# First FFT of a filter-and-FFN kernel: both banks of a stage A pair filled ahead of their copies, four units of F placed ahead of stage B, W_out behind z on the queue

## The chip, the core and the metric

One core of a Trainium2 chip. The metric is the device time of one execution in microseconds (us), as the median of several runs. A "span" is the time from the first to the last instruction of one profiled execution; it is 1 to 2 us shorter than the device time. The program runs on one core only. Ratios are the mean time of one kernel's fast runs over the mean time of the fast runs of the kernel before in the same rounds, with a 95% interval. They are therefore not quite the ratio of the medians that are quoted beside them. Different calls ran on different chips, so medians of different calls are compared only roughly.

Names in the views: tiles that begin with ps lie in PSUM (psA, psT, psB, psP, psY: stage A, the transposes, stages B, P and Y; psf: F being spread; psH, psO: the FFN's first and second product). uT and ut are stage A's result before and after the transposes, ze the copies of stage P's result, dZ is z in DRAM, zt is z as it is read back, xw is x. A slot is one step of the FFN loop; a y unit is one of the pieces in which stage Y is done.

## The reference

```python
def _attn_ref(x, filt_r, filt_i):            # x: (8, 3008, 256), filt: (1505, 256)
    X = np.fft.rfft(x, axis=1)
    Y = X * (filt_r + 1j * filt_i)[None]
    return np.fft.irfft(Y, n=3008, axis=1)

def _moe_ref(x, w_in, w_out):                # x: (24064, 256), w_in: (256, 2048)
    h = np.maximum(x @ w_in, 0.0)
    return h * h @ w_out
```

The output of the first is the input of the second. The FFT along 3008 = 64 x 47 points is done by matmuls in stages. Stage A transforms along 47, stage B along 64. The product with the filter F follows, then the inverse stage P, whose result z goes through DRAM to be rearranged, then the inverse stage Y. The FFN then reads y.

## The kernel before

The FFTs of batches 1 to 7 are woven into the FFN loop of the batch ahead of them. The FFT of batch 0 can't be: it stands alone ahead of the loop, with the loads of the weights and the first loads of batch 1. The change touches only this prologue. Its parts, with cuts marked by "...":

```python
p_prod = ctx.enter_context(tc.tile_pool(name="p_prod", bufs=3))
...
sPF = p_prod.tile([128, 6, 128], F16, tag="prod", name="sPF")   # the placement matrix of F
...
def chunk_a0(c):                                   # stage A of batch 0
    for k in range(2):
        banks, groups = bank_pair(...)             # psH: one tile of two banks; psF, psO: two tiles
        for dt in range(2):
            ps = banks[dt]
            for i in range(4):
                ...                                # two matmuls of 96 columns
            ...                                    # then the copy of this bank to uT
...
for c in (0, 2, 1, 3):
    chunk_a0(c)
...                                                # casts of F on GpSimd, casts of W_in
for k in range(6):
    turn_u(k)                                      # transposes psT, copies to ut
    if k > 2:
        place_f(0, k - 3, ...)                     # F spread over the partitions, in psH
place_f(1, 0, nc.scalar)
for r in range(14):
    if r < 12:
        unit_b(0, r)                               # stage B into psF, product with F (VectorE)
    ...                                            # the other eight place_f, on ScalarE
    if r >= 2:
        unit_p(0, r - 2)                           # stage P, copy to ze; every third: write of z
    for k in {4: (0, 1), 7: (2,)}.get(r, ()):
        load_wide(1, k)                            # x of batch 1, 1 MB each
        cast_wide(1, k, nc.gpsimd, nc.gpsimd)
    if r == 10:
        read_z(0, 0, (0,))                         # first half of the z that y units 0 to 3 need
        load_wout(0)                               # 1 MB
        for k in range(2):
            cast_wout(k, nc.gpsimd)
read_z(0, 0, (1,))                                 # the second half: needs all four z writes
read_z(0, 1)
for c in (0, 2, 1):
    chunk_a(1, c)                                  # stage A of batch 1
load_wout(1)
...
for n in range(4):
    unit_y(0, n)                                   # stage Y; the FFN loop starts after it
```

All DMAs shown are issued from one sequencer (SP), in program order: what stands behind a DMA that has to wait, waits too.

## Time and profile before

| | before |
|---|---|
| device time, median of the first 4 runs | 817.5 us (814.8 to 818.6) |
| span of the profiled run | 817.4 us (this execution took 819.15 us) |
| TensorE busy | 785.9 us (96%) |
| FFN loop starts (first psH matmul) | 65.55 us |
| the FFN's first second product (first psO matmul) | 77.4 us |
| last z write issued, landed | 49.69, 60.19 us |

The prediction shows the lines that carry the argument. One more view belongs beside them, the timeline of the DMA queue's sequencer (start, us, engine and line, destination<-source, number of issues). "Landed" times, here and below, are the trace's own records of when a DMA's completion semaphore reached its full count.

```profile
36.95 0.38 SPq L471 DMA_DIRECT2D dZ<-ze  x1
37.43 1.25 SPq L220 DMA_DIRECT2D xw<-in_x_dram  x2
40.50 0.38 SPq L471 DMA_DIRECT2D dZ<-ze  x1
45.42 0.33 SPq L220 DMA_DIRECT2D xw<-in_x_dram  x1
45.84 0.39 SPq L471 DMA_DIRECT2D dZ<-ze  x1
48.46 0.34 SPq L484 DMA_DIRECT2D zt<-dZ  x1
48.89 0.75 SPq L316 DMA_DIRECT2D wout<-in_moe_w_out_dram  x1
49.69 4.25 SPq L471 DMA_DIRECT2D dZ<-ze  x1
60.21 1.25 SPq L484 DMA_DIRECT2D zt<-dZ  x3
```

The reader is to see the order: the loads of x right behind the first z write, and W_out between the third z write (45.84) and the last.

### The profile page before, as it was taken

The numbers are of one execution on the slowest core, as the hardware profiler recorded it, in microseconds if no ns is written. First come the engines' busy times: TensorE is split into PE (matmuls) and PEld (weight loads), VectorE is DVE, ScalarE is ACT, GpSimd is POOL, SyncE is SP. The second block draws the span as 40 slices with busy tenths as digits, with TensorE's granted clock in tenths as the row PEclk, the third lists the DMA queues.
The fourth block names the chain that finished last, engine by engine and source line by source line (L and its number), as shares of the span: only waits on it lengthen the run. The fifth ranks groups of instructions, "written<-read, shape, count | busy, mean of one in ns | idle before, by whom it ended". The sixth has DMA issues, their size and how long they took to land.

```text
span 817.4 us, 14776 instructions
## 1 busy us (share of the span) xinstructions
PE 785.9 (96%) x6102; PEld 554.1 (68%) x6102; DVE 552.7 (68%) x896; ACT 554.1 (68%) x709; POOL 21.9 (3%) x26
## 2 busy tenths in 40 slices
PE   7858899999999999999999999999999999999998
PEld 4734666667767676776668667776767667676666
DVE  5744699459965699557985599656995579653442
ACT  2736576677767677676776767777776767766663
POOL 3330000000000000000000000000000000000000
PEclk9998999999999999999999999999999999999999
DMA  9686356445572555424572455715555242421111
GB/s 365 230 251 176 123 142 163 96 109 165 146 174 59 162 155 138 121 78 142 155 198 62 108 167 145 175 59 163 152 142 116 78 142 79 118 63 39 40 40 52
DMA packets 88092, 108.10 MB, mean 132 GB/s; under 512 B 6241, under 2 KB 78817, under 8 KB 83553
## 3 DMA queue, kind: packets, MB, share of 16 engines
q1 hardware_dynamic: 87816, 107.01, 46.2%
q8 instruction: 48, 0.79, 0.4%
q10 hardware_dynamic: 144, 0.15, 0.1%
q14 instruction: 20, 0.16, 0.1%
q0 software_dynamic: 64, 0.00, 0.0%
HBM read 58.90 MB, written 48.23 MB: 131 GB/s over the span
## 4 chain that ended last, share of the span: by engine, by line
PE 85%; DMA 9%; DVE 3%; ACT 2%; issue 0%; POOL 0%; SPq 0%; ACTq 0%; POOLq 0%
PE psO L547 36%; PE psH L532 35%; DMA dZ<-ze 3%; DMA zt<-dZ 3%; PE psY L502 3%; PE psA L349 3%; PE psB L431 2%; PE psP L466 2%; DMA ut<-dU 1%; DMA xw<-in_x_dram 1%; DVE prod L434 1%; PE warm L267 1%; DVE h L540 1%; PE psf L283 0%; PE psf L286 0%; PE psA L392 0%
## 5 line engine op out<-in xcount | busy, mean ns | idle before, releaser
L536 ACT ACTIVATE h<-psH 128x1024 f16<-128x1024 f32 x376 | 384.9, 1025 | 193.8 <-PE psH L532 193.8
L532 PE MATMUL psH<-yt,sWin 128*128 128x512 f16 (+7 forms) x1728 | 388.3, 352 | 2.9 <-DVE yt L511 2.3
L547 PE MATMUL psO<-sWout,h 128*128 128x256 f16 x3008 | 388.6, 272 | 0.0
L547 PEld LDWEIGHTS <-h 128*128 128x128 f16 x3008 | 290.6, 98 | 77.8
L540 DVE TENSOR_TENSOR h<-h 128x1024 f16<-128x1024 f16 x376 | 254.2, 685 | 106.3 <-ACT h L536 104.9
L532 PEld LDWEIGHTS <-sWin 128*128 128x128 f16 x1728 | 159.7, 98 | 104.0 <-issue 6.4
L434 DVE TENSOR_TENSOR prod<-psB,sF 128x1024 f16<-128x1024 f32 x96 | 116.7, 1220 | 10.4 <-PE psB L431 7.2
L511 DVE CAST yt<-psY 128x376 f16<-128x376 f32 x64 | 35.0, 549 | 63.3 <-PE psY L502 57.5
L468 ACT CAST ze<-psP 128x512 f16<-128x512 f32 x96 | 55.9, 585 | 22.8 <-PE psP L466 19.4
L355 DVE CAST u<-psA 96x512 f16<-96x512 f32 x50 | 34.3, 687 | 47.9 <-PE psA L349 45.1
L554 ACT COPY ost<-psO 128x512 f32<-128x512 f32 x94 | 55.4, 590 | 8.1 <-PE psO L547 6.4
L502 PE MATMUL psY<-sC,zt 112*128 112x94 f16 x512 | 42.8, 207 | 8.0 <-DMA zt<-dZ 7.7
L502 PEld LDWEIGHTS <-zt 112*128 112x128 f16 x512 | 35.1, 99 | 20.3 <-DMA zt<-dZ 7.7
L431 PE MATMUL psB<-ut,sSB 128*128 128x256 f16 x192 | 36.6, 272 | 2.3 <-DVE prod L434 1.2
L448 DVE TENSOR_TENSOR yf<-prod,yf 128x512 f16<-128x512 f16 x84 | 35.7, 425 | 2.9
L349 PE MATMUL psA<-x,sC 94*96 94x512 f16 x96 | 36.6, 382 | 0.0
L509 ACT CAST yt<-psY 128x376 f16<-128x376 f32 x64 | 29.9, 468 | 7.5 <-issue 6.5
L431 PEld LDWEIGHTS <-sSB 128*128 128x128 f16 x192 | 18.6, 98 | 23.5 <-issue 4.8
L466 PE MATMUL psP<-yf,sSP 128*128 128x256 f16 x168 | 32.1, 273 | 1.8 <-DVE prod L434 1.6
L328 DVE CAST x<-x 94x2048 f16<-94x2048 f32 x24 | 29.2, 1216 | 0.0
L353 ACT CAST u<-psA 96x512 f16<-96x512 f32 x50 | 28.6, 572 | 0.0
L441 DVE COPY yf<-prod 64x512 f16<-64x512 f16 x84 | 24.3, 290 | 2.9
(59 smaller groups left out, 231.6 us busy)
## 6 DMA issues: line engine op xcount, KB each, us to landing
x<-in_x_dram SPq DMA_DIRECT2D x20, 768.0 KB
dZ<-ze SPq DMA_DIRECT2D x32, 384.0 KB
zt<-dZ SPq DMA_DIRECT2D x64, 192.0 KB
dU<-u SPq DMA_DIRECT2D x28, 384.0 KB
out_dram<-ost SPq DMA_DIRECT2D x32, 256.0 KB
out_dram<-ost SPq DMA_DIRECT2D x64, 128.0 KB
ut<-dU SPq DMA_DIRECT2D x7, 1024.0 KB
xw<-in_x_dram SPq DMA_DIRECT2D x6, 1024.0 KB
```

Source lines behind the costliest of these rows:

```text
L349: nc.tensor.matmul(ps[0:96, :], sSA, x16s[(b, c)][:, m, :], start=True, stop=True)
L431: nc.tensor.matmul(ps[:, i * D:(i + 1) * D], sSB[:, 2 * p + i, :], uts[b][:, 2 * p + i, :], start=True, stop=True)
L434: nc.vector.tensor_mul(out=prod, in0=ps.rearrange("p (a d) -> p a d", d=D).unsqueeze(1).to_broadcast([128, 2, 2, D]), in1=sF[:, :, 2 * p:2 ...
L448: nc.vector.tensor_add(out=yf, in0=prod[:, 0], in1=yf)
L466: nc.tensor.matmul(ps[:, i * D:(i + 1) * D], sSP[:, c2, :], prod[:, i, :], start=True, stop=True)
L468: nc.scalar.copy(out=zes[(b, c)][:, 2 * i6:2 * i6 + 2, :], in_=ps.rearrange("p (a d) -> p a d", d=D))
L502: nc.tensor.matmul(ps[:, 94 * jj:94 * jj + 94], zt[:, 4 * (g % 2) + jj, dt * 128:(dt + 1) * 128], sSY, start=True, stop=True)
L532: nc.tensor.matmul(ps[:, i, o:o + n], sWin[:, dt, jt * 128:(jt + 1) * 128], yts[b][:, dt, r:r + n], start=(dt == 0), stop=(dt == 1))
L536: nc.scalar.activation(out=h2[:, 2 * s:2 * s + 2, :], in_=ps, func=AF.Relu)
L540: nc.vector.tensor_mul(out=v, in0=v, in1=v)
L547: nc.tensor.matmul(pso[g][:, t % 2, :], h2s[g][:, jt, t * 128:(t + 1) * 128], sWout[:, jt, :], start=(jt == 0), stop=(jt == NJT - 1))
L554: nc.scalar.copy(out=ost, in_=pso[g])
```

## The change

It has three parts. **Banks:** in stage A of batch 0 all matmuls of a pair come first, then its two copies. **F:** the transposes 4 and 5 use the smaller PSUM tiles so that psH is free for F, four units of F are placed after the transposes and ahead of stage B (three before; these are units of F's real part, and one of its imaginary part is placed there in both kernels), f_i and the identity matrix are loaded earlier, and VectorE takes one of the casts of F. **Queue:** the first load of batch 1's x is issued ahead of stage B, and W_out is loaded after the last z read that the first y units need, with all its casts on VectorE. The core of the diff (the new column numbers of the constants are left out):

```diff
-    nc.sync.dma_start(out=sPF, ...); nc.sync.dma_start(out=sC0[:, 576:1472], ...)
-    load_f(1)
+    load_f(1)
+    nc.sync.dma_start(out=sPF, ...); nc.sync.dma_start(out=sC0[:, 704:1472], ...)
@@ chunk_a0
             for dt in range(2):
-                ps = banks[dt]
                 for i in range(4):
                     ...                                    # matmuls into banks[dt]
+            for dt in range(2):
                 ...                                        # copy of banks[dt]
@@ turn_u
+        if k > 3:
+            npair[0] = k - 2                               # psF, psO in place of psH
@@ W_out's casts in the FFN loop
-            for k in range(2, 4):
-                put(2 + k, 1, cast_wout, k, nc.vector)
+            for k in range(4):
+                put(3 + k, 1, cast_wout, k, nc.vector)
@@ prologue
     for k in range(6):
         turn_u(k)
-        if k > 2:
-            place_f(0, k - 3, nc.vector if k % 2 else nc.scalar)
+    nc.vector.tensor_copy(out=f16s[0][:, 1, e1], in_=f32s[1][:, e1])
+    for k in range(4):
+        place_f(0, k, nc.vector if k % 2 else nc.scalar)
     place_f(1, 0, nc.scalar)
+    load_wide(1, 0)
+    cast_wide(1, 0, nc.gpsimd, nc.gpsimd)
     for r in range(14):
         ...
-        for k in {4: (0, 1), 7: (2,)}.get(r, ()):
+        for k in {4: (1,), 7: (2,)}.get(r, ()):
             ...
         if r == 10:
             read_z(0, 0, (0,))
-            load_wout(0)
-            for k in range(2):
-                cast_wout(k, nc.gpsimd)
     read_z(0, 0, (1,))
+    for k in range(2):
+        load_wout(k)
     read_z(0, 1)
     for c in (0, 2, 1):
         chunk_a(1, c)
-    load_wout(1)
```

Lines behind the change have numbers higher by two in the new kernel: the product is L434 before and L436 after.

More of the change, by code (lines that the diff above doesn't have):

```diff
@@ L103, in _build_consts @@
     C0[:, 0:576] = S0.reshape(128, 6, 2, 2, NC).transpose(0, 1, 4, 2, 3).reshape(128, 576)
-    C0[:, 896:1472] = S0.reshape(128, 576)
-    C0[0:94, 576:672] = SA.reshape(94, 96)
-    C0[:, 672:766] = SY.reshape(128, 94)
-    C0[:, 768:896] = np.eye(128)
+    C0[:, 576:704] = np.eye(128)
+    C0[:, 704:1280] = S0.reshape(128, 576)
+    C0[0:94, 1280:1376] = SA.reshape(94, 96)
+    C0[:, 1376:1470] = SY.reshape(128, 94)
     return f16(C0, 128), f16(PF, 128), f16(SB, 128), f16(SP, 128), f16(SPx, 128)
@@ L203 @@
     sC0 = const.tile([128, 1472], F16, name="sC0")
-    nc.scalar.dma_start(out=sC0[:, 0:576], in_=dC0.ap()[:, 0:576])
+    nc.scalar.dma_start(out=sC0[:, 0:704], in_=dC0.ap()[:, 0:704])
     s0 = sC0[:, 0:576].rearrange("p (w q) -> p w q", q=96)
-    s1 = sC0[:, 896:1472].rearrange("p (w q) -> p w q", q=96)
-    sSA = sC0[0:94, 576:672]
-    sSY = sC0[0:112, 672:766]
-    ident = sC0[:, 768:896]
+    s1 = sC0[:, 704:1280].rearrange("p (w q) -> p w q", q=96)
+    sSA = sC0[0:94, 1280:1376]
+    sSY = sC0[0:112, 1376:1470]
+    ident = sC0[:, 576:704]
     sPF = p_prod.tile([128, 6, 128], F16, tag="prod", name="sPF")
@@ L243 @@
     load_f(0)
+    load_f(1)
     nc.sync.dma_start(out=sPF, in_=dPF.ap().rearrange("p (w q) -> p w q", q=128))
-    nc.sync.dma_start(out=sC0[:, 576:1472], in_=dC0.ap()[:, 576:1472])
-    load_f(1)
+    nc.sync.dma_start(out=sC0[:, 704:1472], in_=dC0.ap()[:, 704:1472])
     nyq = p_out.tile([128, 2, D], F32, tag="ost", name="nyq")
@@ L386, in chunk_a0 @@
             for dt in range(2):
-                ps = banks[dt]
                 for i in range(4):
                     m = 4 * k + i
-                    o = ps[:, 96 * i:96 * i + 96]
+                    o = banks[dt][:, 96 * i:96 * i + 96]
                     d = slice(128 * dt, 128 * dt + 128)
@@ L395, in chunk_a0 @@
                                      start=False, stop=True)
+            for dt in range(2):
                 m = 32 * c + 16 * k
                 o = uT[:, dt, :, m:m + 16].rearrange("p c (m q) -> p m c q", q=4)
-                pv = ps[:, 0:384].rearrange("p (m c q) -> p m c q", m=4, q=4)
+                pv = banks[dt][:, 0:384].rearrange("p (m c q) -> p m c q", m=4, q=4)
                 if (pair_engine() is nc.scalar) if len(groups) == 1 else (dt == 0):
@@ L638 @@
     f16s.append(p_h2.tile([128, 2, QF + D], F16, tag="h2", name="f16"))
+    e0, e1 = slice(0, 1504), slice(1504, QF)
     for im in range(2):
         nc.gpsimd.tensor_copy(out=f16s[0][:, im, QF:], in_=nyq[:, im, :])
-        for e in (slice(0, 1504), slice(1504, QF)):
-            nc.gpsimd.tensor_copy(out=f16s[0][:, im, e], in_=f32s[im][:, e])
+    for im, e in ((0, e0), (0, e1), (1, e0)):
+        nc.gpsimd.tensor_copy(out=f16s[0][:, im, e], in_=f32s[im][:, e])
     for k in range(2):
@@ L655 @@
             place_f(1, r // 2 + 1, nc.scalar)
-        if r < 6 and r % 2 == 1:
-            place_f(0, r // 2 + 3, nc.scalar)
+        if r in (1, 3):
+            place_f(0, r // 2 + 4, nc.scalar)
         if r >= 2:
             unit_p(0, r - 2)
-        for k in {4: (0, 1), 7: (2,)}.get(r, ()):
+        for k in {4: (1,), 7: (2,)}.get(r, ()):
             load_wide(1, k)
```

## The prediction

> **What bounds the kernel now.** The page's time slices come first (row 2: TensorE and the clock it was granted, 40 slices of 20.4 us each).
>
> ```profile
> PE   7858899999999999999999999999999999999998
> PEclk9998999999999999999999999999999999999999
> ```
>
> TensorE is full from the fifth slice on; its idle time lies in the first four. The second view, busy time by stretches, puts numbers on that (columns: stretch, length, busy us of PE, PEld, DVE, ACT, POOL, then clock, DMA share, GB/s).
>
> ```profile
> 10.48:20.10 9.62, 6.78 (x130) 6.06 (x128) 5.16 (x9) 3.83 (x8) 5.12 (x5) 1.00 1.01 418
> 20.10:30.00 9.90, 7.90 (x93) 7.01 (x94) 6.31 (x7) 5.14 (x6) 3.68 (x3) 1.00 0.97 395
> 30.00:47.50 17.50, 14.95 (x137) 12.23 (x136) 13.93 (x12) 14.67 (x20) 5.22 (x6) 1.00 0.56 175
> 47.50:58.00 10.50, 6.89 (x25) 3.42 (x24) 3.13 (x4) 3.23 (x5) 4.05 (x4) 0.84 0.95 273
> 58.00:65.50 7.50, 2.05 (x22) 1.94 (x23) 1.30 (x3) 0.94 (x2) 2.02 (x2) 0.75 0.63 137
> 77.50:817.40 739.90, 728.26 (x5619) 515.41 (x5616) 508.34 (x838) 516.10 (x656) 0.00 (x0) 1.00 0.43 118
> ```
>
> The FFN loop starts at 65.5. From 77.5 on TensorE is busy 728.3 of 739.9 us, and the change leaves that code alone. So the end moves one for one with the moment the FFN loop starts, and that moment is what I predict. The chain of waits, in order of time (start, us, what), says what sets it.
>
> ```profile
> 36.95 0.38 SPq L471
> 37.43 0.48 SPq L220
> 38.02 9.50 DMA xw<-in_x_dram
> 47.65 1.05 POOL xw L227
> ...
> 49.69 10.50 DMA dZ<-ze
> 60.21 3.19 DMA zt<-dZ
> 63.45 0.49 PE psY L502 x4
> ```
>
> Before 36.95 the chain runs through TensorE and the copies of stages A and B; after it, it is a queue. The loads of batch 1's x are issued at 37.43 because they stand behind the first write of z (L471) in the queue's program order; from 31 to 37 us the DMA moved 0 GB/s in each microsecond. Then the last write of z, issued at 49.69 behind 1 MB of W_out (48.89), lands at 60.2, and the read of z takes 3.2 us more. TensorE sits idle 5.5 us for it. Last, the timeline of TensorE in stage A:
>
> ```profile
> 11.56 0.20 PE L392 MATMUL psA<-sC,xw 128*128 128x96 f16 x1 [0.57 <-ACT uT L400]
> 13.09 0.20 PE L392 MATMUL psA<-sC,xw 128*128 128x96 f16 x1 [0.65 <-DVE uT L402]
> ```
>
> In a pair held by one two-bank tile the matmuls of the second bank wait for the copy of the first.
>
> **What the Trainium skill says.** "PSUM — Partial Sum Buffer", Summary: rules for kernel authors, asks a reader of PSUM beside a running matmul to use a different bank. The two halves here are different banks, so the 0.57 and 0.65 us are waits of the tile's bookkeeping, not ones the chip needs; filling both first removes them. "DMA: Bandwidth & Descriptors", Two DMAs through the same engine are not ordered, says that only the completion semaphore orders a read behind a write; so z is paid as a full landing and then a read. The trace agrees: the first z write, on an idle DMA, took from 36.95 to 40.25, the read from 60.21 to 63.4. "TensorE: Matmul & The Clock Gate", Part 1, says that an idle window of about 3.4 us halves the clock. Here the clock records show half speed from 48.1 to 51.5 and 61.7 to 68.6, after the two long TensorE gaps.
>
> **The change, part by part.** Order of instructions by engine confirms what follows; the hand schedule uses durations of the trace.
>
> Stage A. A pair is 16 matmuls at 45 ns, 0.72 us, eight pairs 5.8 us. Copies are 0.48 us (ACT) and 0.56 us (DVE), two per pair on alternating engines, so a pair's 1.0 to 1.1 us of copying covers two pairs of matmuls, and three sets of PSUM buffers rotate: TensorE no longer waits. It starts at 10.48 as before (the second x load, cast by 10.05, sets that), ends at 16.3, and the last copies at 17.1. The transposes psT then begin at 17.1 in place of 20.1: **3.0 us earlier**.
>
> Transposes and F. Six transposes of 0.44 us; the last two now take the smaller banks and wait there for copies of 0.6 to 0.68 us, so TensorE passes them at about 20.9. f_i is loaded ahead of the small constants, so it lands near 18.5 in place of 20.9, and POOL has only three casts of 1.41 us; DVE takes the fourth (about 1.0 us from 0.69 us per 1024 columns), at 22.0 to 23.0 behind its transposes' copies. A placement is 8 to 10 matmuls at 0.11, about 0.9 us, with a copy of 1.02 (ACT), 1.22 (DVE) or 1.11 (ACT, signed). Two PSUM buffers alternate, so the chain is place 0 (21.8), its copy (22.9), DVE's cast and copy of place 1 (24.3), place 3 (25.2), the signed one (26.1) and its copy (27.3). The first product can start at **27.3 in place of 29.7**, and with one more unit placed.
>
> Stage B. Twelve products at 1.2 us are 14.4 us of DVE. ACT has 7 placements and 12 copies of 0.58 us, 14.5 us; TensorE 7 x 0.95 + 7.9 = 14.6. I walk the rounds: the last product ends at 41.9, the last z copy at **43.0 in place of 47.4**; the first three z copies of groups end near 34.8, 37.6 and 40.4.
>
> Queue. The first x load no longer stands behind z: it is issued when POOL has cast the first half of W_in (29.14 + 2.02 = 31.2), not at 37.4. On the busy DMA, landings of the fast engines were spaced 3.0 us for 1 MB of x, 1.1 for a z write, 0.9 for a z read, 3.5 for a W_out half. So x0 lands at 36.5, z0 at 37.5, x1 at 40.5, z1 at 41.5; x2 needs x0's buffer (cast done 38.6) and ends at 44.5, z2 at 45.6, the first z read at 46.6, z3 at 47.7. The slowest engine lagged the others by 2 to 4 us in this stretch (x2: first 50.6, last 54.6); with about 3 us, z3 counts as landed at 50.5. The read of 3.2 us follows: **zt at 53.7, not 63.4**. Batch 1's stage A fits in between (three chunks of 1.75 us, x2 cast about 48). W_out now comes after. Four y units then take the same 2.1 us, and the FFN starts near 55.8: **9.7 us gained**.
>
> Given back. The z read for y units 4 to 7 now stands behind 2 MB of W_out: 52.7 + 3.5 + 3.5 + 1.9 = 61.6, landed about 62.5. It was used 5.4 us into the FFN, which would be 61.2. So a wait of about **1.2 us**. DVE also gets two more W_out casts (2 x 0.69 us) before the second product of the FFN, but in 12 us it has only 5.5 + 2.8 + 1.1 us to do. Sum: 9.7 - 1.2 = 8.5; 817.2 - 8.5 = 808.7, say 808.5.
>
> **Rivals.** First, everything shows: stages A and B gain 4.4 us, the queue the rest, the lag of the slow DMA engine falls to 1 us and z lands with its copies (43.0 + 3.3 + 3.2 = 49.5). The FFN starts at 51.6 and the time is about 803. For it: W_out no longer stands between. Against: about 3 MB of x and z is squeezed into the same few microseconds. Second, stages A and B are hidden: the z chain is bound by the queue, and a lag of 4 us or a slow x2 leaves z at 53 and zt at 56; time about 811. Third, W_out becomes the wait: its two halves land after 61, the zt reads after 64, and the FFN's first group stalls 3 us or more; about 811 to 813. Fourth, DVE becomes the bound of the first FFN slots (square 0.69, cast 0.69, half a y copy 0.27 in a slot of 1.4); it costs a microsecond at most.
>
> **Range and chances.** The second and third rivals stack to about 813.5; the first alone gives 803. Faster by 2% needs 800.9, an FFN start near 49.2, earlier than even the first rival, so 0.05. Slower by 2% has no mechanism: 0.01.
>
> **What would show it.** Right: psT from about 17, no wait of TensorE for a copy of uT inside stage A, the first product near 27.3, the first x load of batch 1 issued near 31.2, no DMA hole of 6 us, the last z write issued near 43.5, psY of the first y unit near 53.7, and the half clock once more there. Wrong: psY near 49 or 57 (the lag was mis-sized), products spaced more than 1.3 us (stage B bound by TensorE or ACT), the DVE cast of f_i waiting for its load, or a wait for zt or W_out in the first eight FFN slots above 3 us. An idle TensorE after 80 us that was not there before would break the one-for-one rule.

## The result

The changed kernel takes 807.8 us (median of 4 runs, 806.9 to 809.5), against 817.5 us before. The ratio is 0.9889 (0.9859 to 0.9918), which is 9.1 us less: the same within 2%, and clear of noise. The output is correct. The profiled run's span is 806.2 us.

The page's time slices of the changed kernel, rows 2 (TensorE, and its granted clock):

```profile
PE   8879899999999999999999999999999999999997
PEclk9999999999999999999999999999999999999999
```

The third and fourth slices, 5 and 8 before, are now 7 and 9, the first is 8 in place of 7, and the fourth slice of the clock is back at 9. From the fifth slice to the last but one nothing has moved. The busy time by stretches of the changed kernel (columns as in the prediction):

```profile
10.48:17.00 6.52, 6.52 (x132) 6.01 (x130) 4.12 (x9) 3.48 (x8) 3.95 (x5) 1.00 1.04 438
...
27.00:43.00 16.00, 13.93 (x126) 11.47 (x125) 12.77 (x11) 12.85 (x17) 7.38 (x8) 1.00 0.81 281
43.00:50.00 7.00, 6.19 (x32) 3.66 (x33) 3.87 (x5) 4.39 (x7) 2.75 (x3) 1.00 0.66 222
```

Stage A is full of matmuls now (6.52 of 6.52 us; stage A starts at 11.08 in this execution, behind the last warm-up matmuls). Stage B, 27 to 43, has TensorE busy 13.9 of 16 us, about as before. The chain of waits of the changed kernel, in order of time, runs through the last z write and the z reads to a wait in the FFN's first slots:

```profile
44.42 0.62 PE psP L465 x4
45.07 0.59 ACT ze L470
45.68 3.45 DMA dZ<-ze
49.20 0.31 SPq L486
...
52.12 8.59 DMA zt<-dZ
...
60.85 0.33 PE psY L504 x4
```

The last z write is no longer behind other transfers for long: it is issued right after the last copy of z (45.66) and takes 3.45 us, where it took 10.5. The queue's sequencer shows why. In the changed kernel:

```profile
31.11 0.33 SPq L220 DMA_DIRECT2D xw<-in_x_dram  x1
35.18 0.38 SPq L473 DMA_DIRECT2D dZ<-ze  x1
...
45.68 0.38 SPq L473 DMA_DIRECT2D dZ<-ze  x1
49.20 0.31 SPq L486 DMA_DIRECT2D zt<-dZ  x1
49.60 1.00 SPq L316 DMA_DIRECT2D wout<-in_moe_w_out_dram  x2
```

The first load of x goes at 31.11, not 37.43, and W_out comes after the z read of 49.20. The FFN starts at 54.32. The chain's last lines show what was given back: the z read of y units 4 to 7, issued behind 2 MB of W_out, lands at 60.7 and TensorE waits for it in the FFN's fourth slot. The waits of TensorE by what ended them, from 53 to 67 us of the changed kernel (total us, times, longest; the first line of two):

```profile
PE psY L504 <- DMA zt<-dZ: 1.4, 1, 1.4
```

### The profile page after: what moved, and what is told of

Its sections match the earlier page's. It is cut to its first block, busy times and chain, and to the rows that moved or that the text cites. A ratio compares the mean times of both kernels' runs of the same rounds, so it can differ in the third digit from the quotient of the medians.

```text
span 806.2 us, 14778 instructions
## 1 busy us (share of the span) xinstructions
PE 784.3 (97%) x6102; PEld 552.4 (69%) x6102; DVE 554.1 (69%) x899; ACT 554.0 (69%) x709; POOL 18.5 (2%) x23
## 4 chain that ended last, share of the span: by engine, by line
PE 87%; DMA 6%; DVE 4%; ACT 1%; issue 0%; SPq 0%; ACTq 0%; DVEq 0%
PE psO L549 37%; PE psH L534 36%; DMA zt<-dZ 3%; PE psA L349 3%; PE psB L433 3%; PE psY L504 2%; DMA ut<-dU 2%; PE psP L468 2%; DVE prod L436 2%; DMA dZ<-ze 1%; PE warm L267 1%; PE psf L283 1%; ACT h L538 0%; PE psf L286 0%; DVE h L542 0%
## 5 line engine op out<-in xcount | busy, mean ns | idle before, releaser
L436 DVE TENSOR_TENSOR prod<-psB,sF 128x1024 f16<-128x1024 f32 x96 | 116.6, 1219 | 10.9 <-PE psB L433 7.4
L470 ACT CAST ze<-psP 128x512 f16<-128x512 f32 x96 | 55.8, 585 | 22.8 <-PE psP L468 19.4
L504 PE MATMUL psY<-sC,zt 112*128 112x94 f16 x512 | 42.8, 207 | 5.2 <-DMA zt<-dZ 5.2
```

The lines of the kernel that those rows point to most:

```text
L436: nc.vector.tensor_mul(out=prod, in0=ps.rearrange("p (a d) -> p a d", d=D).unsqueeze(1).to_broadcast([128, 2, 2, D]), in1=sF[:, :, 2 * p:2 ...
L470: nc.scalar.copy(out=zes[(b, c)][:, 2 * i6:2 * i6 + 2, :], in_=ps.rearrange("p (a d) -> p a d", d=D))
L504: nc.tensor.matmul(ps[:, 94 * jj:94 * jj + 94], zt[:, 4 * (g % 2) + jj, dt * 128:(dt + 1) * 128], sSY, start=True, stop=True)
```

## The experiments

To compare runs, the prologue is cut at six events, all read from each run's trace: the first matmul of stage A, the first transpose (psT), the first product with F, the end of the last z copy, the landing of the last z write, and the first psO matmul of the FFN. The last is the safest yardstick, since what is given back in the FFN's first slots lies ahead of it. From there to the end it was 738.4 to 740.3 us in all fourteen traces. Stage A itself starts between 9.6 and 11.1 us, differently in each execution, so lengths between events say more than absolute times. The rows "after" and "again" are the same kernel.

| run | stage A to psT | psT to first product | first product to last z copy | last z copy at | last z write: issue to landing | landed | first psO at | ratio |
|---|---|---|---|---|---|---|---|---|
| before | 9.20 | 10.02 | 17.73 | 47.43 | 10.50 | 60.19 | 77.38 | 1 |
| after | 6.13 | 10.72 | 17.73 | 45.66 | 3.45 | 49.13 | 66.80 | 0.9889 |
| e1 banks only | 6.13 | 10.02 | 17.73 | 44.65 | 9.74 | 56.84 | 74.32 | 0.9960 |
| e2 queue only | 9.19 | 10.02 | 17.72 | 46.88 | 3.19 | 50.09 | 67.70 | 0.9909 |
| e3 after without banks | 9.19 | 10.71 | 17.73 | 48.74 | 3.77 | 52.53 | 70.15 | 0.9923 |
| e4 after, 3 product buffers | 6.13 | 10.72 | 15.59 | 42.77 | 5.03 | 49.52 | 67.41 | 0.9886 |
| e5 early x load only | 9.20 | 10.02 | 17.72 | 47.18 | 7.39 | 54.59 | 71.14 | 0.9938 |
| e6 W_out behind z only | 9.19 | 10.02 | 17.73 | 47.13 | 6.15 | 55.10 | 74.33 | 0.9974 |
| e7 after, z reads first | 6.13 | 10.72 | 17.73 | 45.64 | 3.11 | 48.78 | 64.46 | 0.9871 |
| e8 both e4 and e7 | 6.44 | 11.11 | 15.60 | 42.76 | 5.70 | 49.97 | 66.77 | 0.9885 |
| e9 F only | 9.56 | 10.72 | 17.73 | 47.69 | 10.60 | 59.98 | 76.68 | 0.9995 |
| e10 banks and queue, no F | 6.13 | 10.02 | 17.73 | 44.24 | 5.41 | 49.68 | 67.42 | 0.9888 |
| e11 e10, z reads first | 6.15 | 10.00 | 17.73 | 43.76 | 5.25 | 49.03 | 65.63 | 0.9866 |
| e12 again | 6.13 | 11.19 | 17.73 | 44.70 | 3.77 | 48.49 | 66.09 | 0.9888 |

The theory after reading the two traces was that z lands when its copies do (account 1), against the prediction's own view that the DMA queue sets it (account 2). All outputs are right.

**e1, the banks alone** (kernel before plus this):

```diff
             for dt in range(2):
-                ps = banks[dt]
                 for i in range(4): ...
+            for dt in range(2):
                 ...  # copy
```

> The kernel before with stage A's banks filled ahead alone. If stage A is on the path that sets the FFN's start (my account), the first x load of batch 1, which follows the first z write, comes with it: transposes from 17.1 to 17.7, first product 2 to 3 us earlier than 29.7, FFN start near 63 in place of 65.55, time 2 to 3 us shorter. If the part is hidden behind loads (f_i or the z chain), psY stays at 63.4 and the time within 0.5 us.

Measured: 814.7 us, ratio 0.996 (0.9936 to 0.9983), 3.3 us less. From stage A to the first transpose it is 3.07 us shorter; every later event up to the FFN's start comes about 3 us earlier (62.25 in place of 65.55). The part works on the path even with the old queue, because the first x load follows the first z write. The waits of TensorE in stage A, before and then after, name what went:

```profile
PE psA L392 <- DVE uT L402: 1.3, 2, 0.7
PE psA L392 <- ACT uT L400: 1.1, 2, 0.6
```

```profile
PE psT L412 <- ACT uT L400: 0.2, 1, 0.2
```

**e2, the queue alone** (kernel before plus this):

```diff
+    load_wide(1, 0); cast_wide(1, 0, ...)        # ahead of stage B
-    W_out: first half at r == 10, second behind stage A of batch 1
+    W_out: both behind read_z(0, 0, (1,)), four casts on VectorE in the FFN loop
```

> The kernel before with the queue's part alone (first x load ahead of the z writes, W_out behind z). Account 1, z lands when its copies do (copies end, write 3.45, read 3.2, as in the changed kernel's trace): copies end at 47.4 as before, z3 lands near 50.9, psY near 54.1, FFN start near 56.1, against 54.3 in the changed kernel; 1.8 us slower than the changed kernel, about 9.5 us faster than before. Account 2, the DMA queue sets it (as I predicted): psY at 52.4 and the time of the changed kernel.

Measured: 809.7 us, ratio 0.9909 (0.989 to 0.9928), 7.4 us less. The last z copy was at 46.88, the write took 3.19 us, psY began at 53.45, which is account 1 shifted by its earlier copy (46.88 + 3.2 + 3.3 = 53.4). The time fell short of the 9.5 us that account 1 gave. So at this setting z moves with the copies; whether through the last write's own copy or through the third x load, which moves with them too, is taken up at e4.

**e3, the changed kernel without the banks** (the inverse of e1's edit on the changed kernel).

> The changed kernel with stage A's copies back after each bank. Account 1 (copies set z): transposes from 20.1, first product, last z copy, psY and FFN start each about 2.5 us later (30.4, 48.1, 54.9, 56.8). Account 2 (the queue sets z): first product later by 2.5 us, but psY within 0.5 us of 52.4.

Measured: 811.3 us, ratio 0.9923 (0.9905 to 0.9942). Last z copy 48.74, landing 52.53, psY 55.87: 3.1 to 3.4 us later than in the changed kernel. Again z moves with the copies.

**e4, a third buffer for the products.** The pool of products has three buffers, but the placement matrix sPF lies in one of them until the last placement:

```diff
-    sPF = p_prod.tile([128, 6, 128], F16, tag="prod", name="sPF")
+    sPF = p_u.tile([128, 6, 128], F16, tag="u", name="sPF")
```

> The changed kernel with the placement matrix sPF held in a free buffer of the u pool, so that stage B's products rotate through three buffers and not two. If the two buffers are what stretched twelve products of 1.2 us to 16.4 us, the waits of DVE for psP (2.0 us in four) go, the last product ends near 42.5 in place of 44.4 and the last z copy near 44. Account 1: psY 1 to 1.7 us earlier (near 51), time about 1.5 us shorter. Account 2: the copies earlier, psY still at 52.4. Third: TensorE's own order of work sets the pace of stage B, and the last copy stays at 45.6.

Measured: 808.0 us, ratio 0.9886 (0.9866 to 0.9906), so no gain against the changed kernel. Yet the edit did what it should. VectorE's waits in stage B of the changed kernel, and then of e4:

```profile
DVE prod L436 <- PE psP L465: 2.0, 4, 0.7
...
```

```profile
DVE prod L436 <- ACT sF L293: 1.0, 1, 1.0
DVE prod L436 <- PE psB L433: 0.3, 1, 0.3
```

The wait for psP, which frees a product's buffer, is gone, stage B is 2.1 us shorter, and the last z copy is at 42.77. But z landed at 49.52, no earlier than before. The queue's sequencer in e4:

```profile
44.09 0.34 SPq L486 DMA_DIRECT2D zt<-dZ  x1
44.48 0.42 SPq L473 DMA_DIRECT2D dZ<-ze  x1
49.58 0.31 SPq L486 DMA_DIRECT2D zt<-dZ  x1
```

The last z write stood 1.7 us behind a z read that had to wait for the second z write's landing (44.03), and then took 5.03 us beside the third x load (landed 46.86). Here account 2 holds. In the seven runs that have both the queue's part and the banks, z landed at 48.5 to 50.0 wherever the last copy lay between 42.8 and 45.7; where the copies came later (e2, e3), it followed them. The landing records of the traces say more: in all nine runs with the whole queue part z landed 2.5 to 2.8 us behind the third x load (46.45 and 49.13 in the changed kernel, 46.86 and 49.52 in e4, 50.01 and 52.53 in e3). In e4, e8, e10, e11 and e12 the time from the last copy to the landing ranges from 3.8 to 7.2 us, while this distance stays within 2.6 to 2.8. In the changed kernel, e2, e3 and e7 the third x load is itself issued 0.48 us behind the second z write, so it comes with the copies, and there the two accounts can't be told apart.

**e5 and e6, the queue's part in halves** (kernel before plus the early x load, and kernel before plus W_out behind z).

> The kernel before with only the first x load of batch 1 moved ahead of stage B. x0 issued near 31.1, x2 near 41; the first W_out half (1 MB, 3.5 us) still stands ahead of the last z write, whose copies end at 47.4: z3 lands near 54, psY near 57.5, time about 6 us shorter than before. If the early x load is worthless (x was hidden anyway), time within 1 us of before.

> The kernel before with only W_out moved behind z. x0 still at 37.4, so x2 and the z writes behind it are late: z3 lands near 56.5, psY near 60, time 3 to 3.5 us shorter. With e5 this adds up to 9.5 us if the two parts are independent; if W_out alone was what delayed z, this one shows most of the gain (8 us or more) and e5 little.

Measured: e5 812.7 us, ratio 0.9938 (0.992 to 0.9956), 5.1 us less; e6 816.0 us, ratio 0.9974 (0.9954 to 0.9994), 2.1 us less. Together that is 7.2 us, against 7.4 us for both in e2. At the first psO matmul the gains are 6.2 and 3.1 us, together 9.3, against 9.7 in e2. Within the intervals (about 1.5 us each way) the parts add up. Both gains in time were below what was expected (about 6, and 3 to 3.5). For e6 the reason was half wrong too: psY came already at 58.6, 4.9 us earlier than before, but the read of z behind W_out gave back part of it. The wait for it was 2.68 us in one place, and from the FFN's start to the first psO matmul it was 14.3 us in place of 11.8; a half clock, from 67.97 to 71.38, lies in it. The queue's sequencer in e5, then in e6:

```profile
45.43 0.88 SPq L316 DMA_DIRECT2D wout<-in_moe_w_out_dram  x1
47.20 0.36 SPq L471 DMA_DIRECT2D dZ<-ze  x1
54.61 1.25 SPq L484 DMA_DIRECT2D zt<-dZ  x3
```

```profile
45.14 0.33 SPq L220 DMA_DIRECT2D xw<-in_x_dram  x1
...
48.95 0.62 SPq L471 DMA_DIRECT2D dZ<-ze  x1
55.16 0.31 SPq L484 DMA_DIRECT2D zt<-dZ  x1
```

In e5 the last z write has W_out in front of it, in e6 the late x.

**e7, all z reads of y units 0 to 7 ahead of W_out** (on the changed kernel):

```diff
     read_z(0, 0, (1,))
+    read_z(0, 1)
     for k in range(2):
         load_wout(k)
-    read_z(0, 1)
```

> The changed kernel with the z reads of y units 4 to 7 ahead of W_out too. The wait of 1.44 us for zt at 60.85 should go; the casts of W_out come later but DVE has room. If that wait costs the path, time 0.7 to 1.4 us shorter than the changed kernel; if W_out turns into the wait (second half after 61), TensorE waits in FFN slots 8 or 9 and the time is the same or longer.

Measured: 807.4 us, ratio 0.9871 (0.9847 to 0.9895). The wait for zt in the FFN's slots is gone, and from the FFN's start to the first psO matmul it is 10.8 us in place of 12.5. But this profiled execution shows no half clock near the FFN's start, while the changed kernel's has one until 56.13, so the 1.7 us are not the reads' place alone. e7's four runs fall into two pairs: 805.5 and 806.2 us with a mean granted clock of 0.999 and 1.000, 808.6 and 808.7 us with 0.996. The interval overlaps that of the changed kernel, so this needed the same rounds; see e11.

**e8, e4 and e7 together.**

> Both of the two cures on the changed kernel: third product buffer and all of the first z reads ahead of W_out. If each works and they add, 2 to 3 us shorter than the changed kernel, FFN start near 53, time near 805. If stage B's gain only turns into a longer wait for the queue, as e7 alone.

Measured: 808.5 us, ratio 0.9885 (0.9864 to 0.9905): the expectation of an added 2 to 3 us failed. The last copy was at 42.76, the last z write waited 1.5 us for its turn and took 5.7 us, z landed at 49.97. The half clock lasted from 49.7 to 56.6 here. That e8 is no better than e7 is within the intervals; that the third buffer buys nothing is what e4 and e8 agree on.

**e9, F alone** (kernel before plus the part on F).

> The kernel before with the part on F alone (four units placed ahead of stage B, transposes 4 and 5 in the smaller banks, f_i and the identity loaded earlier, one cast of f_i on DVE). In the six traces so far the first product comes 10.0 us after the first transpose without this part and 10.7 us with it, and from the first product to the last z copy it is 17.7 us with and without. Account A (the part costs the path 0.7 us): 10.7 and 17.7 here too, psY up to 0.7 us later than in the kernel before, time the same or slower by up to 1 us. Account B (the part is worth something beside the old queue): 10.7 or less and clearly under 17.7, time at least 1 us shorter.

Measured: 816.9 us, ratio 0.9995 (0.9983 to 1.0008). From the first transpose to the first product it is 10.72 us in place of 10.02, and stage B is 17.73 us as everywhere with two product buffers. Account A: the part lengthens the way to the first product by 0.7 us, and stage B does not become shorter for having one placement fewer, which fits the two product buffers as what paces it. psY was at 63.42, where it was before, but stage A had begun 0.8 us earlier in this execution, and the interval of the time is about 1 us each way: whether the old queue hides the 0.7 us is not shown.

**e10, banks and queue without F**, the companion from the other side.

> The change without its part on F: banks filled ahead and the queue's part on the kernel before. Account A: first product 10.0 us after the first transpose in place of 10.7, last z copy 0.7 us earlier counted from there (27.7), FFN's second product 0 to 0.7 us earlier than in the changed kernel of the same call, time equal or up to 1 us shorter. Account B: slower than the changed kernel by 1 us or more.

Measured: 808.2 us, ratio 0.9888 (0.9872 to 0.9905), the same as the changed kernel in the same rounds (e12, 0.9888). Counted from the first transpose the copies ended at 27.7 us in place of 28.9 in e12, but the last z write took 5.41 us in place of 3.77. Of account A the time came true (equal) and the copies too; account B fell. But the FFN's second product, expected 0 to 0.7 us earlier, came 0.6 us later counted from the first transpose (50.9 and 50.3 us): the part on F costs 0.7 us or more on the copies, and z, 2.7 and 2.6 us behind the third x load here too, does not come sooner without it. The part on F is worth nothing here. With a third product buffer it was not taken out, so its worth there stays open.

**e11, e10 with all z reads first.**

> As the run before, with all reads of z for y units 0 to 7 ahead of W_out. The wait of TensorE for zt inside the first FFN slots (1.1 to 2.6 us in the runs that have W_out ahead of them) goes; from the FFN's start to its first second product 10.8 to 11.3 us in place of 12.5. Time 1 to 2 us shorter than the run before and the shortest of this call, near 0.986 of before; if W_out becomes the wait, no gain.

Measured: 806.4 us (805.5 to 807.0), ratio 0.9866 (0.985 to 0.9882), against 808.0 us (807.3 to 808.8) for the changed kernel. The two sets of runs do not overlap. It is some 1.6 us ahead of the changed kernel, and it has one part of the change less. Its ratio is the lowest of all, but e7's, 0.9871, can't be told from it. From the FFN's start to the first psO matmul it was 11.9 us, not the expected 10.8 to 11.3. Those are the values of e7 and e8, where a half clock covered none and 1.1 us of the FFN. In e11 and e12 it covers some 3.4 us at the FFN's start, and there it is 11.9 against 13.0: about 1.1 us for the place of the z reads. No wait for zt is left among TensorE's waits from 53 to 67 us of e11:

```profile
PE psH L532 <- ACT h L536: 0.4, 2, 0.2
PE psH L532 <- ACT yt L509: 0.3, 1, 0.3
PE psH L532 <- DVE yt L511: 0.2, 1, 0.2
```

**e12, the changed kernel again**, the yardstick.

> The changed kernel once more, as the yardstick of this call's rounds: 0.988 to 0.990 of before, first product 10.7 us after the first transpose, last z copy 28.4 us after it, one wait for zt of 1 to 2 us in the FFN's first slots.

Measured: 808.0 us, ratio 0.9888 (0.9872 to 0.9903). The first product came 11.2 us after the first transpose, not 10.7; e8, whose stage A also started early, shows 11.1. The last z copy was 28.9 us after the first transpose, not 28.4, for the same reason. The trace shows the cause: the part on F puts the placement matrix sPF behind f_i on the queue, so that it lands at 20.38 (20.57 in e8, 15.38 in the kernel before), and TensorE's first placement waits for it (0.3 us in e12, 0.2 in e8). Where stage A starts later, as in e4 or the changed kernel, the placement comes after that landing.

## Why the prediction was right, point by point

The time (808.5 predicted, 807.8 measured), the range and the class were right. The sum was right because two of its terms were off in opposite directions, which is luck.

- **One for one with the FFN's start: right.** In the two profiled runs the FFN starts at 65.55 and 54.32, 11.2 us apart, and the spans are as far apart. The medians are 9.7 us apart and the ratio says 9.1: the profiled execution of the kernel before took 819.15 us, 1.6 more than the median, so the two profiles overstate the gain. The start itself was predicted at 55.8.
- **Stage A: right.** Predicted 3.0 us earlier; measured 3.07 us (9.20 to 6.13), alone (e1) and within the change. (The first transpose before is at 19.67; the 20.1 of the prediction is the second.)
- **F: the step was sized right and its worth was not.** Predicted for the first product: 27.3; measured 27.93, with stage A 0.6 us later in that execution. But the text counted "one more unit placed" as an advantage. e9 and e10 show that the part delays the first product by 0.7 us, counted from the first transpose, and shortens nothing after it.
- **Stage B: mis-sized.** The walk took a product to start whenever VectorE and its inputs were free, and put the last z copy at 43.0. It overlooked that sPF holds one of the three product buffers, so that product r waits for TensorE's stage P of product r - 2. From the first product to the last copy it was 17.73 us, and the last copy was at 45.66. With the third buffer (e4) it was 15.59 us, the copy was at 42.77, and the walk's numbers came true.
- **The queue as what sets z: right as a mechanism, mis-sized.** Predicted: the write issued at 43.5, landing 50.5, with a lag of about 3 us of the slowest DMA engine. Measured: issued 45.68, landing 49.13, with a lag of 0.9 us (first part 48.24, last 49.13). With the copies 2.7 us later than walked, the write found the queue nearly done (the third x load landed at 46.45, the z write before it at 47.53) and took 3.45 us. In e4, with copies at 42.8, z landed at 49.52 by the queue, with a lag of 2.3 us: one microsecond from what was predicted. So the last z copy came 2.7 us later than walked and z 1.4 us earlier, and the sum came out.
- **The queue's two moves: right.** Predicted 9.7 us less the given back for the whole; e2 shows 7.4 us for the queue alone, e5 and e6 that the early load brings about 5 us of it and W_out's place 2.
- **Given back: right.** Predicted a wait of 1.2 us for zt; measured 1.44 us. e7 and e11 show that it was avoidable.
- **Rivals.** The first (everything shows) came half true: the lag fell to 0.9 us and z landed 3.5 us after its last copy, but the copies were late; with early copies the queue held z (e4, e8). The second (stages A and B hidden) fell for stage A (e1, e3) and is right for whatever is gained beyond the changed kernel (e4, e10). The third (W_out as the wait) did not come: W_out landed at 55.33 and 59.28, and the wait was the one of 1.44 us above. The fourth (VectorE the bound of the first slots) did not show: no wait of TensorE for VectorE stands in the FFN's first slots of the changed kernel.
- **Half clock: right in this execution, for a reason that holds only in part.** It was predicted once more near the FFN's start; the clock records show half speed from 52.7 to 56.1. The profiled executions of e2 and e7 show none there, with gaps of TensorE ahead of psY of like length (1.84 and 1.82 us, 2.04 in the changed kernel). Nor does half speed follow the long gaps in the trace of the kernel before: 48.09 lies inside a gap of 1.7 us, and the gap of 2.35 us at 53.5 was followed by none. The idle window of about 3.4 us that the prediction cites stands before 61.7, but before neither 48.09 nor 52.72: in the 3.41 us ahead of these TensorE was busy for 1.50 and 1.37 us. In e2 and e7 it was busy for 1.57 us (50.37 to 53.78) and 1.59 us (49.26 to 52.67), and full speed stayed. By these records half speed can follow a stretch that is not idle; where the limit lies they leave open (1.54 us in e6 without it, 1.56 in e4 with it).

Left open: that the write of z takes 5.0 to 5.7 us in some runs with the queue's part and 3.1 to 3.8 in others is put down to the third x load ahead of it, since z lands 2.5 to 2.8 us behind that load whatever the copies do; no run moved the load behind the write, and none moved the z read that holds up the last write in e4 and e8.

## What to carry to other kernels

When a chain ends in a queue, ask of each transfer in it what stands ahead of it in program order and whether that is needed sooner; here two moves of lines in the issue order (with W_out's casts) brought four fifths of the gain when made alone. The banks alone brought 3.3 us, so the gains of the two overlap. When a stage is walked by hand, count the buffers it rotates through, and look for guests in the pool: one borrowed buffer set the pace of a whole stage. And measure a gain at an event behind the place where it could be given back: W_out's move alone brought the FFN's start 5.5 us forward, and the time only 2.

## What the Trainium skill lacked or had wrong

- "DMA: Bandwidth & Descriptors", Where 436 GB/s comes from, says flatly that for transfers between HBM and SBUF the limit of about 358 GB/s per core binds. Its section on measurements has 425 GB/s for 16 MB on one core and gives about 358 as each core's share when both cores of a pair stream. This agrees with that section: one core alone moved 438 GB/s from 10.5 to 17 us of the changed kernel and 418 from 10.5 to 20 us of the kernel before, mostly loads from HBM.
- The same page, Queues, rings and completion order, tells that a DMA is split over up to 16 engines, and names two of them as usually slower, but has no figure for how far these drift apart in a full row. Between the first and the last engine's completion of one DMA it was 0.6 us at the start of the kernel before (first load of x, 5.64 to 6.24), 2.0 us for f_i (18.97 to 20.94) and 4.0 us for the third x load (50.63 to 54.63). An estimate of a landing in a busy stretch needs this term.
- "Runtime: NRT & Kernel Launch", Instruction fetch mechanics, says that instructions are refilled in blocks of 16 KiB over a DMA queue of the sequencer's own. It calls the cost mostly hidden and does not say what a block costs the data on other queues. The trace has packets of 16384 bytes on the instruction queue, each about 1 us long, at 18.04 and 44.56 us of the kernel before, and the lag of the slowest engine grows by 1.1 to 1.4 us across each (from 0.6 to 2.0 us across the first, from 0.8 to 1.9 across the second). Across a third, at 28.18, it stayed at 2.0. That the one causes the other was not tested.
- No page tells that a tile of two PSUM banks makes the matmuls of its second bank wait for the copy of its first; that wait of 0.57 to 0.65 us went in e1, with a correct result, when both banks were filled first.
